# Pooled attention and routed experts on one core: q loaded behind the copies of k and q, row writes behind V's load, one send of maxima on GpSimd, one look at V later

## The chip, the core and the metric

The kernel runs on one core of a Trainium2 chip. The time is device microseconds of one execution. Three runs of the kernel before gave 1505.59, 1509.64 and 1510.80 us, so the median is 1509.64 us. The profile is of one more execution, which took 1513.62 us.

A core has these engines, each with an instruction stream of its own: TensorE (PE, with the weight loads shown apart as PEld), VectorE (DVE), ScalarE (ACT), GpSimd (POOL) and SyncE (SP), which here only issues DMAs. ACT and POOL issue some DMAs too. An engine takes its stream in order: an instruction that waits holds everything behind it.

## The reference

```python
def _attn_ref(q, k, v):                       # 8 batches, 8 heads, 1152 rows, 64 columns
    q_pool = q.reshape(B, H, S // 2, 2, D).mean(axis=3)       # 576 pooled queries
    scores = scale * np.matmul(q_pool, k.transpose(0, 1, 3, 2))
    scores = scores - np.max(scores, axis=-1, keepdims=True)
    attn = np.exp(scores)
    attn = attn / (np.sum(attn, axis=-1, keepdims=True) + 1e-09)
    return np.matmul(attn, v)

def _moe_ref(x, w_gate, w_output_gate, w1, w2):  # 4608 tokens of 512, 8 experts, hidden 1024
    logits = x @ w_gate
    e_idx = np.argmax(logits, axis=1)
    gate_w = softmax(logits)[np.arange(N), e_idx]
    eom = 1.0 / (1.0 + np.exp(-(x @ w_output_gate)))
    for e in range(E):
        mask = e_idx == e
        h = np.maximum(x[mask] @ w1[e], 0.0)
        out[mask] = gate_w[mask, None] * eom[mask, e, None] * (h @ w2[e])
```

Attention makes 4608 token rows. Each row then goes through the one expert that its gate picks.

## The kernel before

**Attention, by pairs.** Two heads of a batch are a pair: there are 32 pairs, four to a batch. The loop over `s` in `attention` takes 18 steps for a pair. In step `s`, TensorE makes the scores of one chunk of 128 keys against 576 queries (`sps`, lines 393 and 395, two accumulating groups), one or two matmuls of the *next* pair for its row maxima (`mp`, line 330), and in some steps a burst of `av` matmuls of an earlier chunk (lines 424 to 426, `ALAG` = 6 steps later). ScalarE takes two exponentials of each `sps` tile, either to `p` and `ph` (lines 407 and 408; GpSimd subtracts them to `pl` on line 409) or to `ph` and back into the tile (lines 399 and 400; VectorE subtracts on line 403). There are two `sps` buffers, so the scores of chunk c+2 wait for the readers of chunk c.

**Maxima.** VectorE reduces each `mp` tile (line 331). The maxima of a pair come in two groups, query tiles 0 to 4 and 5 to 8. A group is transposed by TensorE (line 365), split into two rows `mr` (lines 370, 371), and two small DMAs send these rows into `qb` (`send`, line 376, through `dmaf`, line 125), where the score matmul of line 395 subtracts them. `sends` runs them at the start of a step. Before the change ScalarE's stream issues all of them, 128 in 64 twos.

**Preparation of a pair**, by the tables `PREPF` (pair 0), `PREP0` (pair 1) and `PREP` (the others); a number in a table is a third of a step. `lk` loads q (`qp`, line 150) and k (`kpf`, line 151). GpSimd adds the two q rows that are pooled (`qsum`, line 235, into `yq`); ScalarE rounds k (`xk`, line 229) and q (`xq`, line 238); GpSimd makes the remainders (`kp` line 232, `yq` line 241). Twelve DMAs from SBUF to SBUF then lay these parts out for the matmuls: four `ka` of 288 KB, four `qa` or `qb` from `xq` of 144 KB, two `qa` from `yq` of 144 KB and two `kb` of 288 KB, 2592 KB in all, each of them through `dmaf`. They are called the copies below. `lv` loads V (`vp`, line 225) behind the k load that was issued last. `amax` (line 267, ScalarE) sums the absolute values of V of a head for a scale; `gmax` (line 272, TensorE) adds these over partitions; `vh`, `vs` and `vl` scale and split V into `vt`.

**Order.** PE, DVE, ACT and POOL take their instructions in the order in which the code calls them (`manual_schedule`). SP's order is a scheduler's: it places a DMA by when it thinks that its buffer is free. `qp`, `kpf` and `vp` have one buffer each. The DMAs that SP and ACT issue take eight semaphores in turn, so each such DMA, before it is issued, waits until the one eight places earlier on that list has landed. DMAs that GpSimd issues have eight semaphores of their own.

**Router.** After a batch's fourth pair, `logits` and `router` choose the experts, one piece per step or two. `wr` writes the batch's token rows to DRAM: 512 of them in one DMA of 1026 KB (line 575) and 64 in another of 128 KB (line 576). The index scatter has five parts (`t`), three steps apart; `wr` is called after the third.

**Experts.** Then come tiles of up to 256 tokens of one expert: gather of rows (line 750), `hps` (line 913), `yp` (lines 941 to 946), scatter.

Of the kernel before, what the change touches and what calls it, by code (L numbers as in the profile page):

```python
# [21 lines left out]
LS = 0  # L22
RI = 7
PREP0 = ((0, 'lk'), (6, 'qsum'), (10, 'kh', 0), (11, 'qh'), (12, 'kh', 1), (13, 'ql'), (14, 'kl'), (13, 'dq', 0), (14, 'dq', 1), (17, 'qd'), (21, 'sk', 0, 0), (24, 'sk', 0, 1), (27, 'sk', 1, 0), (30, 'sk', 1, 1), (23, 'dl', 0), (24, 'dl', 1),
        (53, 'lv'), (71, 'amax', 0), (74, 'amax', 1), (81, 'gmax'), (82, 'scale', 0), (85, 'scale', 1), (90, 'scale', 2), (93, 'vh', 0), (93, 'vs', 0), (96, 'vh', 1), (97, 'vl', 0), (100, 'vs', 1), (104, 'vl', 1))
PREPF = ((0, 'lf'), (1, 'fsel'), (3, 'qsv'), (4, 'kh', 0), (5, 'kh', 1), (6, 'klh', 0), (7, 'klh', 1), (8, 'sk', 0, 0), (9, 'sq0'), (10, 'sk', 0, 1), (11, 'sl', 0, 0), (13, 'qd'),
         (45, 'sl', 0, 1), (46, 'sk', 1, 0), (48, 'sk', 1, 1), (51, 'sq1'), (54, 'sl', 1, 0), (57, 'sl', 1, 1), (56, 'lv'),
         (78, 'amax', 0), (82, 'amax', 1), (99, 'gmax'), (100, 'scale', 0), (100, 'scale', 1), (100, 'scale', 2), (103, 'vh', 0), (103, 'vs', 0), (106, 'vh', 1), (107, 'vl', 0), (109, 'vs', 1), (113, 'vl', 1))
# [38 lines left out]
def attention(tc, qT, kT, vL, wg, keep, xrows, idscr, cum, pairs, setup, scat, init, exps):  # L67
    nc = tc.nc
    nb = len(pairs) // 4
    with ExitStack() as ctx:  # L70
# [51 lines left out]
            VTs.append(vt)  # L122

        def dmaf(o, i, q=nc.sync):
            q.dma_start(out=o.bitcast(F32), in_=i.bitcast(F32))

        lastk, sel, shn = [None], [], [0]

        def prep(n, table):

# [16 lines left out]
            gm = []  # L147

            def lk():
                nc.sync.dma_start(out=qp, in_=qT[b, hp].rearrange("p (t n) -> p t n", t=2))  # L150
                lastk[0] = nc.sync.dma_start(out=kpf, in_=kT[b, hp])


# [68 lines left out]

            def lv():
                with tc.issue_after(lastk[0].ins):
                    nc.sync.dma_start(out=vp, in_=vL[b, hp].rearrange("p (c d) -> p c d", d=64))

            def kh(i):
                z = slice(i * NQ, i * NQ + NQ)
# [30 lines left out]
            def dl(h):  # L259
                r = slice(64 * h, 64 * h + 64)  # L260
                o = h * (NQ + 64)
                dmaf(qa[64:128, o:o + NQ], yq[r])
                dmaf(kb[0:64, h], kp[r])

            def amax(h):
                j = sm.tile([128, NC, 64], F16, name="junk", bufs=1)
# [93 lines left out]
        def rows(force=False):  # L360
            while pend_t and (force or now[0] >= pend_t[0][-1] + TLAG):
                m9, nt, t0, t1, qbf, _ = pend_t.pop(0)
                tp, tk = psum(True)
                tp = tp[0:nt, 0:128]
                nc.tensor.transpose(out=tp, in_=m9[:, 0:nt], identity=ident)
                mr = sm.tile([5, 2, 128], F32R, name="mr")[0:nt]
                c0 = 16.0 * SHIFT

                def split(tp=tp, tk=tk, mr=mr, qbf=qbf, t0=t0, t1=t1, nt=nt):
                    nc.vector.tensor_scalar(out=mr[:, 0], in0=tp, scalar1=c0, scalar2=None, op0=ALU.subtract)  # L370
                    nc.vector.scalar_tensor_tensor(out=mr[:, 1], in0=tp, scalar=c0, in1=mr.bitcast(F32)[:, 0], op0=ALU.subtract, op1=ALU.subtract)
                    free(tk)

                    def send():
                        for j in range(2):
                            dmaf(qbf[66 + j:67 + j, 128 * t0:128 * t1].rearrange("o (t n) -> o t n", n=128), mr[:, j], nc.scalar)
                    pendd.append((send, now[0]))
                if now[0] < 18:
                    split()
                else:  # L380
                    pendv.append(split)
# [125 lines left out]
        def router(b, xb):  # L507
# [64 lines left out]

            def wr():
                r0 = b * NQ
                nc.sync.dma_start(out=xrows[r0:r0 + 512].rearrange("(t p) n -> p t n", p=128), in_=xb[:, 0:4])
                nc.sync.dma_start(out=xrows[r0 + 512:r0 + NQ], in_=xb[64:128, 4])
            if b == nb - 1:
                wr()
# [10 lines left out]
            for t in range(5):  # L589
# [5 lines left out]
                for q in scat:  # L595
                    tc.declare_no_dep(i.ins, q, reason="distinct slots")
                scat.append(i.ins)
                if t == 2 and b < nb - 1:
                    wr()
            if b == max(nb - 3, 0):  # L600
                yield from setup(psum, free)
# [640 lines left out]
```

## Time and profile before

| | |
|---|---|
| runs | 1505.59, 1509.64, 1510.80 us |
| profiled execution | 1513.62 us, span of its instructions 1511.9 us |
| mean granted TensorE clock | 0.987 |
| attention | to about 1000 us of the span, 32 pairs |
| change from attention to experts | about 1000 to 1060 us |
| experts | from about 1060 us to the end |
| largest load of the DMA engines | queue q1 (SP's), 241.52 MB |

The rows of the profile are read as follows. A row of the timeline has start, duration, engine, line, operation, what it writes and reads, and in brackets the engine's idle time before it with what ended it. "SPq" and "ACTq" are DMA issues by SP and ACT, and "x2" there is two of them with whatever lies between. A row of the windows gives, for a stretch of time, the busy time of each engine, the granted TensorE clock and what the DMA engines moved. A row of the waits gives who waited for whom, with total, times and longest.

### The profile page before, as it was taken

To read this page: it belongs to the slowest core of one execution; us is meant where nothing else is said; L and a number is where in the kernel's file an instruction comes from. 1 tells how busy PE (TensorE), PEld (TensorE's weight loads), DVE (VectorE), ACT (ScalarE), POOL (GpSimd) and SP (SyncE) were. 2 spreads that over 40 slices of the span, in tenths; PEclk is the share of its full clock that TensorE was granted. 3 is DMA by queue.
4 is the path that set the end of the run, shared out by engine and by line. 5 is a ranking of instruction groups with operands and counts; after the bars stand their busy time and mean duration, and the time that the engine had idled before them with its cause. 6 is when DMAs were issued, how large, how long until landed. Compare 5 with 4: busy or idle time off the path is not lost.

```text
span 1511.9 us, 40870 instructions
## 1 busy us (share of the span) xinstructions
PE 1469.9 (97%) x15806; PEld 1338.4 (89%) x15806; DVE 1100.0 (73%) x2359; ACT 1123.7 (74%) x1957; POOL 1014.0 (67%) x896
## 2 busy tenths in 40 slices
PE   7999999999999999999999999997999999999998
PEld 6989999999999999999899999985888888888985
DVE  7667777786777677777677777747778777787863
ACT  6778888888888888888788888884556556556662
POOL 5877888888888889878888998887233323333410
PEclk9999999999999999999999999997999999999999
DMA  5567665675566656665557655447966667446761
GB/s 170 137 160 183 164 153 140 164 172 150 135 167 168 157 135 153 173 166 152 136 140 176 168 141 154 101 149 257 354 235 214 227 234 234 164 174 240 254 218 67
DMA packets 96659, 265.95 MB, mean 176 GB/s; under 512 B 12778, under 2 KB 17018, under 8 KB 96450
## 3 DMA queue, kind: packets, MB, share of 16 engines
q1 hardware_dynamic: 85994, 241.52, 57.0%
q0 software_dynamic: 9024, 20.85, 3.9%
q8 instruction: 128, 2.10, 0.6%
q10 hardware_dynamic: 1440, 0.89, 0.2%
q14 instruction: 73, 0.60, 0.1%
HBM read 164.23 MB, written 22.50 MB: 124 GB/s over the span
## 4 chain that ended last, share of the span: by engine, by line
PE 91%; DVE 4%; ACT 2%; DMA 1%; POOL 1%; issue 1%; ACTq 0%; POOLq 0%; DVEq 0%; SPq 0%
PE mp L330 20%; PE hps L913 14%; PE sps L393 11%; PE sps L395 10%; PE av L424 6%; PE av L425 6%; PE av L426 6%; PE yp L943 4%; PE yp L944 4%; PE yp L946 4%; DVE pm L331 2%; PE tp L479 1%; PE xps L892 1%; PE tp L496 1%; PE yp L941 1%
## 5 line engine op out<-in xcount | busy, mean ns | idle before, releaser
L331 DVE TENSOR_REDUCE pm<-mp 128x1 f32<-128x384 f32 x864 | 452.4, 550 | 218.3 <-PE mp L330 217.3
L409 POOL TENSOR_TENSOR pl<-p,ph 128x576 f16<-128x576 f32 x386 | 494.1, 1286 | 153.0 <-ACT ph L408 119.8
L407 ACT ACTIVATE p<-sps 128x576 f32<-128x576 f32 x386 | 252.8, 655 | 104.6 <-PE sps L395 62.6
L330 PE MATMUL mp<-ka,qa 128*128 128x384 f32 x960 | 315.4, 345 | 0.0
L424 PEld LDWEIGHTS <-ph 128*128 128x128 f16 x2880 | 263.2, 97 | 39.7 <-issue 30.1
L424 PE MATMUL av<-vt,ph 128*128 128x65 f16 x2880 | 296.5, 194 | 0.0
L425 PE MATMUL av<-vt,ph 128*128 128x64 f16 x2880 | 294.4, 195 | 0.0
L426 PE MATMUL av<-vt,pl 128*128 128x65 f16 x2880 | 293.5, 193 | 0.0
L393 PE MATMUL sps<-qa,ka 128*128 128x288 f32 x1152 | 279.6, 324 | 10.9 <-ACT ph L408 7.0
L425 PEld LDWEIGHTS <-ph 128*128 128x128 f16 x2880 | 266.0, 97 | 0.8
L426 PEld LDWEIGHTS <-pl 128*128 128x128 f16 x2880 | 266.3, 99 | 0.0
L330 PE MATMUL mp<-kb,qb 66*128 66x384 f32 x768 | 261.3, 340 | 0.9 <-DVE kb L204 0.6
L408 ACT ACTIVATE ph<-sps 128x576 f16<-128x576 f32 x386 | 251.4, 651 | 0.0
L395 PE MATMUL sps<-qb,kb 68*128 68x288 f32 x1152 | 248.2, 297 | 0.0
L913 PE MATMUL hps<-x,w1h 128*128 128x512 f32 (+2 forms) x704 | 223.3, 381 | 2.1 <-DVE x L897 2.1
L393 PEld LDWEIGHTS sps<-qa,ka 128*128 128x128 f32 x1152 | 184.9, 192 | 15.7 <-ACT ph L408 9.9
L395 PEld LDWEIGHTS sps<-qb,kb 68*128 68x128 f32 x1152 | 187.0, 191 | 0.0
L330 PEld LDWEIGHTS mp<-ka,qa 128*128 128x128 f32 x960 | 179.0, 191 | 1.7 <-DVE pm L331 1.5
L913 PE MATMUL hps<-x,w1l 128*128 128x256 f32 (+2 forms) x704 | 162.6, 272 | 0.0
L915 ACT COPY hs<-hps 128x512 f32<-128x512 f32 (+2 forms) x88 | 47.4, 538 | 152.8 <-PE hps L913 144.4
L403 DVE TENSOR_TENSOR pl<-sps,ph 128x576 f16<-128x576 f32 x190 | 143.5, 755 | 16.9 <-ACT sps L400 12.9
L399 ACT ACTIVATE ph<-sps 128x576 f16<-128x576 f32 x190 | 124.4, 655 | 40.2 <-PE sps L395 31.6
(258 smaller groups left out, 2933.4 us busy)
## 6 DMA issues: line engine op xcount, KB each, us to landing
ka<-xk SPq DMA_DIRECT2D x120, 288.0 KB
raw1b<-in_w_dram SPq DMA_DIRECT2D x24, 1024.0 KB
raw2b<-in_w_dram SPq DMA_DIRECT2D x24, 1024.0 KB
raw1a<-in_w_dram SPq DMA_DIRECT2D x22, 1024.0 KB
raw2a<-in_w_dram SPq DMA_DIRECT2D x22, 1024.0 KB
vp<-in_vL_dram SPq DMA_DIRECT2D x32, 576.0 KB
qp<-in_qT_dram SPq DMA_DIRECT2D x31, 576.0 KB
kpf<-in_kT_dram SPq DMA_DIRECT2D x31, 576.0 KB
```

The lines of the kernel that those rows point to most:

```text
L330: nc.tensor.matmul(mp, lhsT=l, rhs=r, start=j == 0, stop=j == len(ops) - 1)
L331: nc.vector.tensor_reduce(out=pm[:, i:i + 1], in_=mp, axis=AX.X, op=ALU.max)
L393: nc.tensor.matmul(sps[:, j, 0:288], lhsT=ka[:, h, ks], rhs=qa[:, o + 288 * j:o + 288 * j + 288], start=True, stop=False)
L395: nc.tensor.matmul(sps[:, j, 0:288], lhsT=kb[:, h, ks], rhs=qb[:, h, 288 * j:288 * j + 288], start=False, stop=True)
L403: nc.vector.tensor_tensor(out=pl.rearrange("p (j n) -> p j n", j=2), in0=x, in1=ph2, op=ALU.subtract)
L407: nc.scalar.activation(out=p32.rearrange("p (j n) -> p j n", j=2), in_=x, func=AF.Exp, scale=1.0 / 16)
L408: e_ = nc.scalar.activation(out=ph2, in_=x, func=AF.Exp, scale=1.0 / 16)
L409: nc.gpsimd.tensor_tensor(out=pl, in0=p32, in1=ph, op=ALU.subtract)
L424: nc.tensor.matmul(av_[:, qb, 0:65], lhsT=hi, rhs=vt[:, h, c, 0:65], start=c == 0 and qb == 0, stop=False)
L425: nc.tensor.matmul(av_[:, qb, 0:64], lhsT=hi, rhs=vt[:, h, c, 66:130], start=False, stop=False)
L426: nc.tensor.matmul(av_[:, qb, 0:65], lhsT=lo, rhs=vt[:, h, c, 0:65], start=False, stop=c == NC - 1 and qb == 4)
L913: nc.tensor.matmul(hp[:, f, 0:n], lhsT=W1[l][g][:, c, fs], rhs=d['x'][:, c, 0:n], start=c == 0 and l == 0, stop=c == 3 and l == 0)
```

## The change

Five edits. `lk` issues q's load only after the last copy (`kb`) of the pair before it in the preparation. `wr` issues the write of 512 rows only after the V load that was called last, for all batches but the last, and is called after the fifth part of the scatter rather than the third. The send of maxima for query tiles 5 to 8 is issued by GpSimd when it comes up before step 9, which is so for pair 0 alone. In `PREP0`, the two `amax` of pair 1 come five thirds of a step later. The rest keeps the handles that this needs.

```diff
 PREP0 = (...
-        (53, 'lv'), (71, 'amax', 0), (74, 'amax', 1), (81, 'gmax'), (82, 'scale', 0), ...
+        (53, 'lv'), (76, 'amax', 0), (79, 'amax', 1), (81, 'gmax'), (82, 'scale', 0), ...
...
         def dmaf(o, i, q=nc.sync):
-            q.dma_start(out=o.bitcast(F32), in_=i.bitcast(F32))
-
-        lastk, sel, shn = [None], [], [0]
+            return q.dma_start(out=o.bitcast(F32), in_=i.bitcast(F32))
+
+        lastv = [None]
+        lastk, lastl, sel, shn = [None], [], [], [0]
...
             def lk():
-                nc.sync.dma_start(out=qp, in_=qT[b, hp].rearrange("p (t n) -> p t n", t=2))
+                with tc.issue_after(lastl[0].ins) if lastl else ExitStack():
+                    nc.sync.dma_start(out=qp, in_=qT[b, hp].rearrange("p (t n) -> p t n", t=2))
                 lastk[0] = nc.sync.dma_start(out=kpf, in_=kT[b, hp])
...
             def lv():
                 with tc.issue_after(lastk[0].ins):
-                    nc.sync.dma_start(out=vp, in_=vL[b, hp].rearrange("p (c d) -> p c d", d=64))
+                    lastv[0] = nc.sync.dma_start(out=vp, in_=vL[b, hp].rearrange("p (c d) -> p c d", d=64))
...
                 dmaf(qa[64:128, o:o + NQ], yq[r])
-                dmaf(kb[0:64, h], kp[r])
+                lastl[:] = [dmaf(kb[0:64, h], kp[r])]
...
                         for j in range(2):
-                            dmaf(qbf[66 + j:67 + j, ...], mr[:, j], nc.scalar)
+                            dmaf(qbf[66 + j:67 + j, ...], mr[:, j], nc.gpsimd if t0 and now[0] < 9 else nc.scalar)
...
             def wr():
                 r0 = b * NQ
-                nc.sync.dma_start(out=xrows[r0:r0 + 512].rearrange("(t p) n -> p t n", p=128), in_=xb[:, 0:4])
+                with tc.issue_after(lastv[0].ins) if b < nb - 1 else ExitStack():
+                    nc.sync.dma_start(out=xrows[r0:r0 + 512].rearrange("(t p) n -> p t n", p=128), in_=xb[:, 0:4])
                 nc.sync.dma_start(out=xrows[r0 + 512:r0 + NQ], in_=xb[64:128, 4])
...
-                if t == 2 and b < nb - 1:
+                if t == 4 and b < nb - 1:
                     wr()
```

The changed file is up to three lines longer, so a line such as 150 is 152 there, and 575 is 578. TensorE's and VectorE's streams hold the same instructions in the same order. The streams of SP, ACT and POOL change.

SP's stream in the first batches, at a pair with no row write beside it. `qp`, `kpf` and `vp` are the loads of q, k and V; the rows between them are the copies of one pair. Before:

```order
L225 DMA vp<-in_vL_dram 128x1152
L150 DMA qp<-in_qT_dram 128x1152
L125 DMA ka_121<-xk_5153 64x1152 x4
L125 DMA qa_124<-xq 64x576
L125 DMA qb_127<-xq 64x576
L125 DMA qa_124<-xq 64x576
L125 DMA qb_127<-xq 64x576
L125 DMA qa_124<-yq 64x576
L125 DMA kb_118<-kp_5149 64x1152
L125 DMA qa_124<-yq 64x576
L125 DMA kb_118<-kp_5149 64x1152
L151 DMA kpf<-in_kT_dram 128x1152
```

And after the change, the same pair:

```order
L227 DMA vp<-in_vL_dram 128x1152
L125 DMA ka_121<-xk_5153 64x1152 x4
L125 DMA qa_124<-xq 64x576
L125 DMA qb_127<-xq 64x576
L125 DMA qa_124<-xq 64x576
L125 DMA qb_127<-xq 64x576
L125 DMA qa_124<-yq 64x576
L125 DMA kb_118<-kp_5149 64x1152
L125 DMA qa_124<-yq 64x576
L125 DMA kb_118<-kp_5149 64x1152
L152 DMA qp<-in_qT_dram 128x1152
L153 DMA kpf<-in_kT_dram 128x1152
```

The load of the following pair's q stood ahead of twelve copies and stands behind them now; k's load keeps its place.

In the pairs where a batch's rows are written (seven of them), q's load stood behind the copies already before the change: there the order was V's load, the write of 512 rows, the copies, the write of 64 rows, q's load, k's load, V's load. After the change it is V's load, the write of 64 rows, the copies, q's load, k's load, V's load, the write of 512 rows.

ScalarE's stream in the first steps, at the second send of pair 0 (`qb_127<-mr`). Before:

```order
L408 ACTIVATE ph<-sps_430 128x576
L125 DMA qb_127<-mr 1x4x128 x2
L399 ACTIVATE ph<-sps_453 128x576
L400 ACTIVATE sps_453<-sps_453 128x2x288
L407 ACTIVATE p_481<-sps_476 128x576
```

After:

```order
L410 ACTIVATE ph<-sps_430 128x576
L401 ACTIVATE ph<-sps_453 128x576
L402 ACTIVATE sps_453<-sps_453 128x2x288
L409 ACTIVATE p_481<-sps_476 128x576
L410 ACTIVATE ph<-sps_476 128x576
```

The two DMAs are gone from here. They stand in GpSimd's stream now, behind the subtraction for chunk 0 (`pl<-p_435,ph`):

```order
L411 TENSOR_TENSOR pl<-p_435,ph 128x576
L125 DMA qb_127<-mr 1x4x128 x2
L411 TENSOR_TENSOR pl<-p_481,ph 128x576
L291 TENSOR_SCALAR vp<-vp,sc 128x576
L294 TENSOR_TENSOR vt_138<-vp,vt_138 128x9x64
```

ScalarE's stream some nine steps later, where the two `amax` of pair 1 (`junk,am<-vp`) stand. Before:

```order
L267 ACTIVATE junk,am<-vp 128x576
L407 ACTIVATE p_710<-sps_705 128x576
L408 ACTIVATE ph<-sps_705 128x576
L267 ACTIVATE junk,am<-vp 128x576
L238 CAST xq<-yq 128x576
L399 ACTIVATE ph<-sps_756 128x576
L400 ACTIVATE sps_756<-sps_756 128x2x288
L125 DMA qb_128<-mr 1x5x128 x2
```

After:

```order
L409 ACTIVATE p_708<-sps_703 128x576
L410 ACTIVATE ph<-sps_703 128x576
L240 CAST xq<-yq 128x576
L269 ACTIVATE junk,am<-vp 128x576
L401 ACTIVATE ph<-sps_754 128x576
L402 ACTIVATE sps_754<-sps_754 128x2x288
L269 ACTIVATE junk,am<-vp 128x576
L125 DMA qb_128<-mr 1x5x128 x2
```

The first moves behind one pair of exponentials and the rounding of q, the second behind the next pair of exponentials.

More of the change, by code (lines that the diff above doesn't have):

```diff
@@ L24 @@
 PREP0 = ((0, 'lk'), (6, 'qsum'), (10, 'kh', 0), (11, 'qh'), (12, 'kh', 1), (13, 'ql'), (14, 'kl'), (13, 'dq', 0), (14, 'dq', 1), (17, 'qd'), (21, 'sk', 0, 0), (24, 'sk', 0, 1), (27, 'sk', 1, 0), (30, 'sk', 1, 1), (23, 'dl', 0), (24, 'dl', 1),
-        (53, 'lv'), (71, 'amax', 0), (74, 'amax', 1), (81, 'gmax'), (82, 'scale', 0), (85, 'scale', 1), (90, 'scale', 2), (93, 'vh', 0), (93, 'vs', 0), (96, 'vh', 1), (97, 'vl', 0), (100, 'vs', 1), (104, 'vl', 1))
+        (53, 'lv'), (76, 'amax', 0), (79, 'amax', 1), (81, 'gmax'), (82, 'scale', 0), (85, 'scale', 1), (90, 'scale', 2), (93, 'vh', 0), (93, 'vs', 0), (96, 'vh', 1), (97, 'vl', 0), (100, 'vs', 1), (104, 'vl', 1))
 PREPF = ((0, 'lf'), (1, 'fsel'), (3, 'qsv'), (4, 'kh', 0), (5, 'kh', 1), (6, 'klh', 0), (7, 'klh', 1), (8, 'sk', 0, 0), (9, 'sq0'), (10, 'sk', 0, 1), (11, 'sl', 0, 0), (13, 'qd'),
@@ L375, in send @@
                         for j in range(2):
-                            dmaf(qbf[66 + j:67 + j, 128 * t0:128 * t1].rearrange("o (t n) -> o t n", n=128), mr[:, j], nc.scalar)
+                            dmaf(qbf[66 + j:67 + j, 128 * t0:128 * t1].rearrange("o (t n) -> o t n", n=128), mr[:, j], nc.gpsimd if t0 and now[0] < 9 else nc.scalar)
                     pendd.append((send, now[0]))
```

## The prediction

> **What bounds the kernel now.** I read the page first, then the windows by stage, then what TensorE waits for, and then ScalarE's and SyncE's timelines at those waits.
>
> ```profile
> span 1511.9 us, 40870 instructions
> PE 1469.9 (97%) x15806; PEld 1338.4 (89%) x15806; DVE 1100.0 (73%) x2359; ACT 1123.7 (74%) x1957; POOL 1014.0 (67%) x896
> PEclk9999999999999999999999999997999999999999
> ...
> 0.00:100.00 100.00, 87.14 (x870) 79.66 (x871) 68.29 (x149) 69.24 (x126) 65.82 (x90) 0.91 0.60 161
> 100.00:1000.00 900.00, 889.16 (x12095) 839.68 (x12091) 668.87 (x1692) 763.04 (x1410) 761.29 (x662) 1.00 0.61 151
> 1000.00:1060.00 60.00, 48.63 (x471) 40.89 (x471) 36.49 (x103) 35.93 (x59) 47.93 (x37) 0.86 0.75 265
> 1060.00:1511.90 451.90, 444.95 (x2381) 378.15 (x2379) 326.32 (x418) 255.51 (x364) 138.94 (x110) 1.00 0.63 217
> ```
>
> TensorE is the bound, and its instructions are the same after the change. So time can come only from its idle time and from stretches at a lower clock. The change reaches the first two rows: 12.9 us idle of the first 100 with a mean clock of 0.91, and 10.8 us idle of the next 900. The stage of the experts is not reached. What ends TensorE's idle time:
>
> ```profile
> PE tp L272 <- ACT junk L267: 2.4, 1, 2.4
> PE sps L393 <- DVE pl L403: 2.3, 3, 1.6
> ...
> PE sps L393 <- ACT ph L408: 6.7, 6, 2.3
> ```
>
> The first two rows are of the first 100 us, the third of 100 to 1000. In all three ScalarE was late. Three of these gaps have a price beyond themselves, since the granted clock is halved behind them:
>
> ```profile
> 30.90:41.10 10.20, 9.88 (x59) 9.32 (x60) 4.64 (x9) 7.15 (x12) 8.29 (x8) 0.50 0.17 57
> 88.90:95.70 6.80, 6.80 (x49) 6.49 (x50) 1.75 (x5) 3.36 (x6) 3.50 (x4) 0.50 0.96 259
> 740.90:744.30 3.40, 3.40 (x36) 3.10 (x37) 0.56 (x1) 2.88 (x5) 3.29 (x3) 0.50 0.99 252
> ```
>
> They stand behind the gaps of 1.6, 2.4 and 2.3 us. The other five gaps of the 6.7 us have 4.4 us together, 0.9 each, and no lower clock behind them. Half-clock time that TensorE fills costs half of its length: 5.1, 3.4 and 1.7 us.
>
> **What makes ScalarE late** is the sends of maxima that it issues:
>
> ```profile
> 27.74 1.30 ACTq L125 DMA_DIRECT2D qb<-mr  x2
> 83.76 3.14 ACTq L125 DMA_DIRECT2D qb<-mr  x2
> 242.10 1.97 ACTq L125 DMA_DIRECT2D qb<-mr  x2
> 736.34 3.26 ACTq L125 DMA_DIRECT2D qb<-mr  x2
> ...
> 334.64 0.70 ACTq L125 DMA_DIRECT2D qb<-mr  x1
> 335.43 0.69 ACTq L125 DMA_DIRECT2D qb<-mr  x1
> ```
>
> A plain send of two takes 1.3 to 1.5 us. At 83.76, 242.10 and 736.34 the second one waited 1.6, 0.5 and 1.8 us longer. It needs the semaphore of the DMA eight places earlier, which is one of the large `ka` copies. SyncE's rows around it:
>
> ```profile
> SPq L150 <- POOL yq L235: 139.6, 23, 7.3
> ...
> 233.18 0.33 SPq L150 DMA_DIRECT2D qp<-in_qT_dram  x1
> 233.61 3.75 SPq L125 DMA_DIRECT2D ka<-xk  x4
> ...
> 245.41 1.34 SPq L151 DMA_DIRECT2D kpf<-in_kT_dram  x1
> ...
> 337.89 1.36 SPq L150 DMA_DIRECT2D qp<-in_qT_dram  x1
> 339.30 0.44 SPq L151 DMA_DIRECT2D kpf<-in_kT_dram  x1
> ...
> 356.99 0.33 SPq L150 DMA_DIRECT2D qp<-in_qT_dram  x1
> ...
> 233.20:245.40 12.20, 11.54 (x137) 10.77 (x135) 9.98 (x27) 9.61 (x20) 9.37 (x9) 1.00 0.95 215
> ```
>
> In 23 pairs q's load sits in SyncE's stream until GpSimd has read the old q, and goes out just ahead of the copies, as at 233.18. It is 576 KB, and the DMA engines then move 215 GB/s, so it holds every copy back by up to 2.7 us. In a pair with a row write, as at 334.64, q goes out after the copies (337.89), and there the two sends stand 0.79 us apart, with no wait between. This case already holds the rearrangement, though with 1026 KB of rows ahead of the copies.
>
> **The change, part by part.**
>
> *q behind the copies.* Removed from ahead of them are 2.7 us of DMA time, more than any of the waits above (1.8 us at most). So the waits go, and with them the 6.7 us of gaps between 100 and 1000 us and the 1.7 us of half clock: **8.4 us**. At 83.76 go the gap of 2.4 us and 3.4 us of half clock, 5.8 us. The second of these sends comes to wait for the fourth `ka` instead of the third, which eats part of the margin, and I take **5.5 us**. Bounds: nothing, if the copies delay one another without q, and 14.2 us together. What is late next: q and k now leave together, at about 245.4 in the pair above. They are 1152 KB, 5.5 us at 215 GB/s, and are used when GpSimd reads q. The rows at 337.89 and 356.99 give the room: the next q is let out 19.1 us after the last one was, behind that read of 1.4 us. So some 12 us are left, and I take nothing for it. Behind q in SyncE's stream stand k's load, which was behind the copies already, and V's load, some 10 us later.
>
> *Row writes.* The rows for this:
>
> ```profile
> SPq L575 <- DVE xb L571: 32.9, 7, 4.7
> ...
> 349.30:357.00 7.70, 7.70 (x125) 7.36 (x122) 5.24 (x13) 6.60 (x14) 7.33 (x8) 1.00 0.27 81
> ```
>
> SyncE waits for the rows' last column as before, 4.7 us each, now with the small write; the copies behind it needed this time anyway, since in a pair without a write they also start about 8 us after V's load. The large write, 1026 KB or 4.9 us at 215 GB/s, moves into the stretch behind V's load, where the DMA engines are at 0.27. It costs nothing, and gains at most the share that it held of the copies' time, which no gap of TensorE shows. If that cover were gone, it would delay the next copies like q did, by 1 to 2 us in seven pairs.
>
> *The second send of pair 0 on GpSimd.* The rows at the start:
>
> ```profile
> 27.39 0.43 PE L395 MATMUL sps<-qb,kb 68*128 68x288 f32 x2
> 29.09 0.65 ACT L399 ACTIVATE ph<-sps 128x576 f16<-128x576 f32 x1 [1.28 <-DVE tp L277]
> 30.31 0.76 DVE L403 TENSOR_TENSOR pl<-sps,ph 128x576 f16<-128x576 f32 x1 [0.39 <-ACT sps L400]
> 31.22 0.82 PE L393 MATMUL sps<-qa,ka 128*128 128x288 f32 x2 [1.55 <-DVE pl L403]
> ...
> 29.10:39.90 10.80, 9.25 (x45) 8.37 (x44) 5.93 (x12) 8.32 (x15) 7.17 (x8) 0.58 0.31 100
> ```
>
> The scores of chunk 1 are there at 27.82, but ScalarE starts on them at 29.09, behind its send. VectorE and TensorE follow in a chain. Without the send this chain is 1.24 us earlier and the gap 0.3 us, so the half clock at 30.9 goes too. Its 5.1 us are not all won. From 29.1 to 39.9 ScalarE has 8.3 us of work. Packed without gaps from 27.85 it ends at 36.2 instead of 39.9. So I take **3.7 us**, with 1.2 (the half clock stays) and 6.4 (all of 1.24 and 5.1) as bounds. GpSimd now issues the two DMAs:
>
> ```profile
> L592 POOL DMA_INDIRECT idscr<-tid,posi x40: 977/1063/1203, 209.0 to 1034.2; - x40
> ...
> 27.89 1.28 POOL L409 TENSOR_TENSOR pl<-p,ph 128x576 f16<-128x576 f32 x1 [4.89 <-ACT ph L408]
> 31.46 1.29 POOL L409 TENSOR_TENSOR pl<-p,ph 128x576 f16<-128x576 f32 x1 [2.29 <-DMA kpf<-in_kT_dram]
> ```
>
> No direct DMA of GpSimd is in the trace. Its indirect ones take 1.06 us, so two take 2.1 us, and GpSimd is idle for 2.29 us there. Bounds are 0 and 2.4 us (two of 1.2). Behind them wait the subtractions `pl`, which TensorE needs six steps later; the rows themselves are needed nine steps later. I take nothing for it.
>
> *V of pair 1 looked at later.*
>
> ```profile
> 48.36 0.69 ACT L267 ACTIVATE junk<-vp 128x576 f16<-128x576 f32 x1
> ...
> 50.12 0.35 PE L272 MATMUL tp<-am,onesf 128*128 128x2 f32 x2
> ```
>
> The second `amax` ends some 1 us ahead of the matmul that sums it, and moves behind two exponentials of 0.55 us each. TensorE may then wait up to 0.8 us there; the exponentials that it overtakes come 0.6 us earlier, which takes away a gap of 0.4 us (the 2.3 us of `pl` above less 1.6 are two such gaps). I take **0.4 us** as a cost (bounds: a gain of 0.4 and a cost of 0.8).
>
> **Sum**, against the profiled 1513.62 us: 8.4 + 5.5 + 3.7 − 0.4 = 17.2 us off, 1496.4 us. The median of the runs, 1509.64, lies 4.0 us below the profiled execution. The gap at 738 us and its half clock, 4.0 us, occur once in the trace and may be just that. They are gone after the change either way, so I keep **1496 us**.
>
> **Rivals.**
>
> *The copies delay one another without q.* Then the sends wait as before and only the start gains: 1513.62 − 3.7 + 0.4 = 1510.3 us. For it: at 242.10 the wait is for the fourth of four copies of 288 KB. Against it: the sends at 334.64 and 335.43.
>
> *The half clock has another cause than these gaps.* Then 1.24 + 2.4 + 6.7 − 0.4 = 9.9 us go and 1503.7 us stay. For it: the half clock at 30.9 begins 0.3 us before the gap's end, so the gap alone need not have set it. Against it: three of three long gaps have it, and five of five short ones don't. [...]
>
> *q comes late (slower).* Where q and k land later than the 12 us of room, GpSimd's sum of q, the copies and then the maxima of the next pair wait, and each microsecond of it counts in 23 pairs: 1496 + 23 = 1519 us for one. From a rate below some 70 GB/s on (1152 KB in 17 us) this decides. For it: two loads now share one slot. Against it: the seven pairs in which they did so already.
>
> *The change doesn't do what it says:* excluded for SyncE's order, which is known.
>
> **How the numbers follow.** The forecast (1490 to 1501 us) has 0.64, the other cause of half clock 0.12, the copies 0.10, q late 0.04. The remaining 0.10 is new short stalls, between 1501 and 1510. The range is 1489 to 1505 us: the forecast with the bounds of its unknown costs, the second rival, and half of the rest. A measurement of this kernel can tell some 0.3%, 4.5 us, from no change, so faster means below 1505.1: 0.64 + 0.12 + 0.05, or 0.81. The same has 0.15 (the copies and the other half of the rest), slower 0.04.
>
> **What would show it.** Right: sends of 1.3 to 1.5 us throughout, TensorE's wait for `ph` L408 between 100 and 1000 us under 1 us, a granted clock of 1.00 from 11 to 1000 us, and no second send in ScalarE's stream near 28 us. Wrong: sends that still take over 1.9 us, GpSimd idle ahead of L235 for q's load, half clock with no gap ahead of it, or a new wait of `sps` or `av` for `pl` in the first 60 us.

## The result, and the profile after

The changed kernel takes 1497.53 us (median of 6 runs, 1493.13 to 1499.76), the kernel before 1510.30 us in the runs beside it. The ratio is 0.9911, with a 95% interval of 0.9892 to 0.9929. The profiled execution took 1499.76 us, 13.9 us less than the profiled one of before.

The page of the changed kernel, and its windows by stage, with the columns as before. The last two rows are the stretch with a lower clock that is left in the attention, and the 3.4 us ahead of it:

```profile
span 1497.9 us, 40864 instructions
PE 1462.9 (98%) x15806; PEld 1331.9 (89%) x15806; DVE 1099.7 (73%) x2359; ACT 1123.0 (75%) x1957; POOL 1015.0 (68%) x898
PEclk9999999999999999999999999998999999999999
```

```profile
0.00:100.00 100.00, 88.76 (x958) 81.32 (x959) 72.97 (x160) 74.54 (x134) 72.29 (x97) 0.97 0.61 163
100.00:1000.00 900.00, 894.00 (x12187) 843.75 (x12186) 668.15 (x1688) 769.07 (x1425) 766.53 (x665) 1.00 0.61 155
...
47.50:54.30 6.80, 6.78 (x59) 6.48 (x60) 3.12 (x8) 3.51 (x6) 2.27 (x4) 0.50 1.03 237
44.10:47.50 3.40, 1.97 (x13) 1.57 (x12) 2.10 (x5) 2.72 (x8) 3.40 (x3) 1.00 0.94 202
```

What TensorE waited for, the first two rows between 0 and 100 us and the others between 100 and 1000:

```profile
PE sps L395 <- DVE pl L405: 1.7, 2, 1.1
PE tp L274 <- ACT junk L269: 1.4, 1, 1.4
...
PE tp L481 <- DVE pm L333: 2.1, 7, 0.3
PE sps L395 <- DVE pl L405: 1.6, 3, 0.7
PE sps L397 <- DMA qb<-mr: 0.5, 1, 0.5
```

The largest row of before, the 6.7 us for `ph` between 100 and 1000 us, is gone, and no stretch at half clock is left there. Still there is a wait for V's sum (`junk`), now at 46 us, and half clock behind it. The sends, from the timeline (the one at 724.82 answers to the one at 736.34 of before):

```profile
21.00 2.10 ACTq L125 DMA_DIRECT2D qb<-mr  x2
...
29.10 1.31 POOL L125 DMA_DIRECT2D qb<-mr  x2
...
63.70 0.62 ACTq L125 DMA_DIRECT2D qb<-mr  x1
...
112.54 0.71 ACTq L125 DMA_DIRECT2D qb<-mr  x1
...
724.82 0.70 ACTq L125 DMA_DIRECT2D qb<-mr  x1
725.61 0.69 ACTq L125 DMA_DIRECT2D qb<-mr  x1
...
981.30 0.60 ACTq L125 DMA_DIRECT2D qb<-mr  x1
```

At 724.82 the second follows the first by 0.79 us, where it came 2.58 us later before. The start of a send also marks the same place of the program in every kernel here, since each has all 64 twos in one order. So the attention is cut into three stretches by four sends: the first of pair 0, the second of pair 1, the first of pair 3 and the last one of pair 31. In the changed kernel these are the sends at 21.00, 63.70, 112.54 and 981.30 us. All kernels of this study, in us of their profiled executions (a profile is one execution), with the median and the ratio from all runs (each ratio is to the kernel before in the runs beside it, whose medians were 1509.33 to 1510.48 us):

| kernel | to pair 1's second send | to pair 3's first | to pair 31's last | median | ratio (95%) |
|---|---|---|---|---|---|
| before | 43.39 | 54.35 | 875.70 | 1510.30 | |
| changed | 42.70 | 48.84 | 868.76 | 1497.53 | 0.9911 (0.9892 to 0.9929) |
| q_only | 43.32 | 48.83 | 865.73 | 1498.60 | 0.9924 (0.9894 to 0.9953) |
| q_ahead | 39.65 | 48.84 | 887.86 | 1513.13 | 1.0027 (1.0005 to 1.0049) |
| send_only | 41.17 | 48.80 | 873.56 | 1506.63 | 0.9983 (0.9969 to 0.9996) |
| amax_back | 43.03 | 48.78 | 866.47 | 1496.26 | 0.9914 (0.9886 to 0.9943) |
| rows_back | 39.51 | 48.86 | 865.93 | 1494.12 | 0.9906 (0.9870 to 0.9943) |
| q_mixed | 41.69 | 48.85 | 866.88 | 1495.27 | 0.9916 (0.9884 to 0.9948) |
| sum_later | 39.11 | 48.85 | 867.37 | 1496.22 | 0.9913 (0.9886 to 0.9941) |
| fill_gap | 39.49 | 48.86 | 867.42 | 1496.01 | 0.9908 (0.9872 to 0.9944) |
| extra_copy | 39.88 | 48.85 | 869.51 | 1498.95 | 0.9920 (0.9898 to 0.9942) |
| sends_pool | 40.08 | 49.64 | 889.23 | 1517.57 | 1.0044 (1.0023 to 1.0065) |
| q_pair3 | 41.23 | 48.97 | 871.56 | 1499.04 | 0.9918 (0.9895 to 0.9941) |
| rows_sum | 39.11 | 48.97 | 867.10 | 1494.88 | 0.9892 (0.9870 to 0.9914) |

Of the 13.9 us between the two profiles, 0.7 lie in the first stretch, 5.5 in the second and 6.9 in the third; the rest lies behind them.

### The profile page after: what moved, and what is told of

Read it like the earlier page. It is cut to its first block, busy times and chain, and to the rows that moved or that the text cites. A ratio compares the mean times of both kernels' runs of the same rounds, so it can differ in the third digit from the quotient of the medians.

```text
span 1497.9 us, 40864 instructions
## 1 busy us (share of the span) xinstructions
PE 1462.9 (98%) x15806; PEld 1331.9 (89%) x15806; DVE 1099.7 (73%) x2359; ACT 1123.0 (75%) x1957; POOL 1015.0 (68%) x898
## 4 chain that ended last, share of the span: by engine, by line
PE 93%; DVE 3%; DMA 1%; issue 1%; ACT 1%; POOL 0%; ACTq 0%; POOLq 0%; SPq 0%; DVEq 0%
PE mp L332 21%; PE hps L916 14%; PE sps L395 12%; PE sps L397 10%; PE av L426 6%; PE av L427 6%; PE av L428 6%; PE yp L946 5%; PE yp L947 5%; PE yp L949 4%; DVE pm L333 1%; PE tp L481 1%; PE xps L895 1%; PE tp L498 1%; PE yp L944 1%
## 5 line engine op out<-in xcount | busy, mean ns | idle before, releaser
L426 PEld LDWEIGHTS <-ph 128*128 128x128 f16 x2880 | 262.6, 97 | 39.5 <-issue 29.2
```

Source lines behind the costliest of these rows:

```text
L426: nc.tensor.matmul(av_[:, qb, 0:65], lhsT=hi, rhs=vt[:, h, c, 0:65], start=c == 0 and qb == 0, stop=False)
```

## The experiments

### q alone behind the copies (q_only)

The kernel before with the edits of `dmaf`, `dl` and `lk`, and nothing else.

```diff
-                nc.sync.dma_start(out=qp, in_=qT[b, hp]...)
+                with tc.issue_after(lastl[0].ins) if lastl else ExitStack():
+                    nc.sync.dma_start(out=qp, in_=qT[b, hp]...)
```

> The kernel before, with one part of the change: the next q loaded behind the copies of k and q. Theory (the q edit carries nearly the whole gain; in the traces the two stretches behind the start gained 5.5 us at 86-94 us and about 7 us at 100-1000 us): 1510.3 - 12.5 = about 1498, ratio 0.990 to 0.993; the first send of pair 1 stays at 50.2 us, the half clock near 31 us stays, TensorE's waits for ph ahead of L393 between 100 and 1000 us are under 1 us in all, and no gap stands near 86 us. The recorded prediction's terms: 8.4 + 5.5 = 13.9 us off, 1496.4. Rival (the copies delay the sends by themselves, and the moved q is not the cause): the gaps of 0.6 to 2.3 us ahead of L393 stay, 1509 to 1511.

It takes 0.9924 of the kernel before, against 0.9911 for all edits. What TensorE waited for `ph` between 100 and 1000 us:

```profile
PE sps L394 <- ACT ph L409: 0.3, 1, 0.3
```

6.7 us in the kernel before are 0.3 us here, and the third stretch is 10.0 us shorter. The start is as before. The q edit carries nearly the whole gain, and the rival falls.

### q ahead again, the other parts changed (q_ahead)

```diff
-                with tc.issue_after(lastl[0].ins) if lastl else ExitStack():
-                    nc.sync.dma_start(out=qp, in_=qT[b, hp]...)
+                nc.sync.dma_start(out=qp, in_=qT[b, hp]...)
```

> The changed kernel with the next q loaded ahead of the copies again; the other three parts stay. Theory (q edit carries the gain): 1497.5 + 12 to 13 = about 1510; waits of 0.6 to 2.4 us ahead of L393 for ph return once in a pair where the sends stand behind the copies, sends take over 1.9 us again. Rival (the row writes or the moved sum of V have a share of it): 1500 to 1506.

The gain is gone: 1.0027, even a little over the kernel before. TensorE's waits between 100 and 1000 us, and from the timeline the send and the gap at 236 us:

```profile
PE sps L394 <- ACT ph L409: 12.2, 9, 2.8
```

```profile
225.24 0.33 SPq L151 DMA_DIRECT2D qp<-in_qT_dram  x1
225.67 3.35 SPq L125 DMA_DIRECT2D ka<-xk  x4
...
236.04 1.83 ACTq L125 DMA_DIRECT2D qb<-mr  x2
237.93 0.65 ACT L408 ACTIVATE p<-sps 128x576 f32<-128x576 f32 x1 [4.23 <-DVE sc L283]
239.17 0.85 PE L394 MATMUL sps<-qa,ka 128*128 128x288 f32 x2 [2.82 <-ACT ph L409]
```

ScalarE starts its exponentials behind the two sends, at 237.93, and TensorE goes on at 239.17. The start, though, took 39.65 us, 3.7 us less than before. So the send's gain is there when q stands ahead. In the third stretch this kernel is 14.3 us longer than send_only. There the edits differ in the row writes alone, but the order on SP differs in q as well. Its waits, here and in the kernel before:

```profile
SPq L151 <- POOL yq L236: 147.3, 29, 7.3
```

```profile
SPq L150 <- POOL yq L235: 139.6, 23, 7.3
```

So q's load stands ahead of the copies in six of the seven pairs that write rows too (send_only has 23 waits, as before). Of the 12.2 us of gaps, 10.7 follow the sends in the last pairs of the batches, whose copies come next behind the moved write; send_only has 4.5 us there.

### The send alone (send_only)

The kernel before with the `send` edit only.

```diff
-    dmaf(qbf[66 + j:67 + j, ...], mr[:, j], nc.scalar)
+    dmaf(qbf[66 + j:67 + j, ...], mr[:, j], nc.gpsimd if t0 and now[0] < 9 else nc.scalar)
```

> The kernel before, with one part of the change: the second maxima of pair 0 sent by GpSimd. Recorded prediction: 3.7 us off (1.2 to 6.4), so 1506.6: the half clock at 30.9 us goes, and TensorE's first score follows 1.2 us earlier. Theory read from the two traces (the start is worth about 4 us by 46 us of the span, and what it loses again lies in the moved sum of V): 1510.3 - 4 = about 1506, first send of pair 1 near 46 us in place of 50.2. Rival (ScalarE, whose sum of V stands early here, now waits for V's load, which does not come earlier by itself): a ScalarE wait of 1 us or more ahead of L269 between 38 and 45 us, a gap of TensorE behind it, and 1509 to 1511.

3.1 us less by the medians (0.9983), and a first stretch that is 2.2 us shorter in the profile. ScalarE's first sum of V, from the timeline:

```profile
45.70 0.69 ACT L267 ACTIVATE junk<-vp 128x576 f16<-128x576 f32 x1 [1.86 <-DMA vp<-in_vL_dram]
```

Both readings are partly right. The send's part is real, and 1.9 us of ScalarE's lead go to a wait for V's load. This kernel also lacks the gap at 86 us, though q stands ahead of the copies in it. q_ahead lacks it too.

### V's sums at their former place (amax_back)

```diff
-        (53, 'lv'), (76, 'amax', 0), (79, 'amax', 1), (81, 'gmax'), ...
+        (53, 'lv'), (71, 'amax', 0), (74, 'amax', 1), (81, 'gmax'), ...
```

> The changed kernel with the sums of V of pair 1 at their former places (71 and 74). Recorded prediction: 0.4 us faster (bounds: 0.8 us faster to 0.4 us slower), 1497.1. Theory A (the moved sum is what cost 1.45 us of gap and 3.4 us of half clock at 46 to 54 us): 1497.5 - 4.9 = 1492.6, no gap ahead of L274. Theory B (V's load lands at 44.9 us whatever the place, so ScalarE would stand waiting for it ahead of its exponentials): same to 2 us slower, 1497.5 to 1499.5, with a wait of ScalarE for the load of 1.5 to 3 us ahead of L269 and a gap of TensorE ahead of L395.

0.9914, the same as the changed kernel. Its timeline, and below it that of the changed kernel at the same place:

```profile
44.80 0.68 ACT L269 ACTIVATE junk<-vp 128x576 f16<-128x576 f32 x1 [2.68 <-DMA vp<-in_vL_dram]
```

```profile
44.92 0.68 ACT L269 ACTIVATE junk<-vp 128x576 f16<-128x576 f32 x1 [0.66 <-DMA vp<-in_vL_dram]
...
46.71 0.67 ACT L269 ACTIVATE junk<-vp 128x576 f16<-128x576 f32 x1
...
47.52 0.59 PE L274 MATMUL tp<-am,onesf 128*128 128x2 f32 x2 [1.45 <-ACT junk L269]
```

The sum starts when V's load lands, at 44.8 and 44.9 us, from both places in ScalarE's stream. Where it stands early, ScalarE waits 2.68 us ahead of it, and TensorE then waits 1.6 us for `ph` in place of 1.45 us for the sum. The half clock from 47.5 us on is in both. So the late load sets this loss, and the place of the sum only chooses who waits.

### The sum's matrix product later (sum_later)

```diff
-        (81, 'gmax'), (82, 'scale', 0), (85, 'scale', 1), (90, 'scale', 2), ...
+        (85, 'gmax'), (86, 'scale', 0), (88, 'scale', 1), (91, 'scale', 2), ...
```

> The changed kernel with the matrix product of V's sums and what follows it (the mask, the scale, the reciprocal) of pair 1 a few steps later (81, 82, 85, 90 become 85, 86, 88, 91); the sums themselves stay at 76 and 79. Theory A (TensorE stands 1.45 us at 46.07 us for the late sum, and half clock follows for 6.8 us): no gap ahead of that product, no half clock near 47 us, second send of pair 1 at 59 to 60.5 us in place of 63.7 (from the first send of pair 0), 1497.5 - 3.5 to 4.9 = 1492.6 to 1494. Rival (the wait moves to the scaled copies of V and to TensorE's product with them): same within 1 us, and a new gap behind 55 us.

The gap and the half clock are gone, and the first stretch is the shortest of all, 39.11 us. From the timeline:

```profile
47.27 0.51 PE L395 MATMUL sps<-qa,ka 128*128 128x288 f32 x2 [0.22 <-DVE pl L405]
...
48.60 0.28 PE L274 MATMUL tp<-am,onesf 128*128 128x2 f32 x2
```

TensorE now has scores to make ahead of the product. The median, 1496.22, is not told apart from the changed kernel's, since V's load came earlier here (the first sum began at 44.41 without a wait), so not all of the 3.6 us are due to this edit.

### One q ahead of nothing (q_mixed)

```diff
-                with tc.issue_after(lastl[0].ins) if lastl else ExitStack():
+                with tc.issue_after(lastl[0].ins) if lastl and n != 2 else ExitStack():
```

> The changed kernel, but the q of pair 2 (the one loaded while pair 1 is made ready) is loaded ahead of the copies again; all later ones stay behind them. Theory (q behind the copies let pair 1's ka copies start at 40.63 us in place of 42.15, beside V's load, which then landed too late for its sum; with q ahead the copies stay out of its way): V's sum without a wait, the gap ahead of the product 0.7 us as in the run with q ahead everywhere, no half clock near 47 us, second send of pair 1 near 60.7 us, later stretches as in the changed kernel: 1497.5 - 3 = 1494.5. Rival (the saving at the start is lost again at 86 us, where the kernel before had its 2.37 us gap): 1497 to 1500, with a half clock near 88 us.

The q of pair 2 was the wrong one. It is loaded at 24 us, ahead of any such copies, so that the order on every engine stays that of the changed kernel. The run tests nothing of the theory and is a second sample of the changed kernel: ratio 0.9916, and a first stretch of 41.69 us in place of 42.70. Its timeline, and its windows cut in stretches of 3.41 us counted from its half clock at 30.9 us, show how a start differs from one execution to the next:

```profile
46.63 0.68 ACT L269 ACTIVATE junk<-vp 128x576 f16<-128x576 f32 x1 [1.39 <-DMA vp<-in_vL_dram]
...
49.22 0.38 PE L274 MATMUL tp<-am,onesf 128*128 128x2 f32 x2 [2.18 <-ACT junk L269]
```

```profile
44.55:47.97 3.42, 2.49 (x21) 2.09 (x17) 1.65 (x5) 2.03 (x6) 3.42 (x3) 1.00 1.02 228
47.97:51.38 3.41, 2.16 (x39) 2.16 (x40) 1.30 (x3) 2.47 (x6) 2.15 (x2) 1.00 0.81 194
51.38:54.80 3.42, 3.22 (x33) 2.98 (x32) 3.19 (x9) 2.76 (x6) 1.69 (x4) 1.00 0.91 214
```

A longer gap, of 2.18 us, has no half clock behind it here (1.00 in all three rows); 0.93 us of it lie in one stretch and 1.25 in the next.

### TensorE kept busy ahead of the product (fill_gap)

Six more products, their result unused, ahead of pair 1's `gmax`.

```diff
+                if n == 1:
+                    f_ = psum(name="fill")
+                    for _ in range(6):
+                        nc.tensor.matmul(f_[:, 0:384], lhsT=ka[:, 0, 0:128], rhs=KAs[0][:, 0, 0:384], start=True, stop=True)
                 nc.tensor.matmul(g, lhsT=onesf, rhs=am, start=True, stop=True)
```

> The changed kernel with six more products (128x384 each, their result unused) on TensorE just ahead of pair 1's product of V's sums, where it stands idle for 1.45 us. Theory (that idle time makes the half clock at 47.5 us): no idle over 0.7 us there, no half clock behind it, second send of pair 1 about 3.4 us earlier than in the changed kernel (60 to 61 us), though the product itself comes no earlier than 47.5; 1497.5 - 3.4 = 1494.1. Rival (the half clock has another cause, and gaps of 1.5 us alone don't bring it): half clock at 47.5 us stays, 1497.5 or up to 1.5 us more.

No gap and no half clock, as the theory has it, but it isn't settled by this: V's load came early in this execution too. From its timeline:

```profile
46.37 0.68 ACT L269 ACTIVATE junk<-vp 128x576 f16<-128x576 f32 x1
...
47.92 1.24 PE L275 MATMUL fill<-ka,ka 128*128 128x384 f32 x6
...
48.99 0.36 PE L278 MATMUL tp<-am,onesf 128*128 128x2 f32 x2
```

Without the fill TensorE would have stood some 1.1 us (47.92 to 48.99), less than the 1.45 us of the changed kernel. That is about as long as in rows_back below, which has no half clock either. Inconclusive.

### The row writes at their former place (rows_back)

```diff
-                with tc.issue_after(lastv[0].ins) if b < nb - 1 else ExitStack():
-                    nc.sync.dma_start(out=xrows[r0:r0 + 512]...)
+                nc.sync.dma_start(out=xrows[r0:r0 + 512]...)
...
-                if t == 4 and b < nb - 1:
+                if t == 2 and b < nb - 1:
```

> The changed kernel with the router's row writes where they were before (at the third of five scatters, both writes ahead of V's load). Recorded prediction: the row writes are worth nothing, 1497.5 with 1 us either way (1496.5 to 1498.5), V's sums in the four pairs behind a batch without a wait. Rival (the large write ahead of V's load and of the copies delays them): 1 to 6 us slower, waits of TensorE for ph between 100 and 1000 us of over 0.6 us near 250, 370, 500 us.

0.9906 against 0.9911, with intervals that overlap, and 865.93 us in the third stretch against 868.76: the moved row writes bring nothing that can be told, and cost some 3 us at most in these profiles. TensorE's waits for `ph` are 0.3 us in all between 100 and 1000 us, so the rival falls. V's load landed earlier in its profile, and the gap ahead of the product was 0.92 us, without half clock:

```profile
47.06 0.38 PE L274 MATMUL tp<-am,onesf 128*128 128x2 f32 x2 [0.92 <-ACT junk L269]
```

Its first write of rows comes only at 188.94 us, so the start is the changed kernel's own, and the first stretch took 39.51 us. So the 42.70 us of the changed kernel are one outcome among several of the same order of instructions at the start.

### Bytes ahead of the copies (extra_copy)

One more copy from SBUF to SBUF, its result unused, ahead of each pair's `ka`.

```diff
+            ex_ = sq.tile([128, 896], F32R, name="extra")
...
+                if h == 0:
+                    dmaf(ex_, xk[:, 0:896])
                 dmaf(ka[0:64, h], xk[r])
```

> The changed kernel with one more copy (448 KB, its result unused) ahead of each pair's copies of k, so that bytes stand ahead of them again though q stays behind; the order of sends and copies on the queues' eight slots is the same. Theory (the sends wait until a ka copy eight transfers earlier has landed, and bytes ahead of the copies make it late): waits of TensorE for ph ahead of L395 between 100 and 1000 us of over 0.6 us again, in four pairs or more, second sends 0.4 us or more behind the first, 5 to 15 us slower than the changed kernel: 1502 to 1512. Rival (it was q's own place, not the bytes): 1496 to 1499.

The sends wait again, but the time hardly follows: 1498.95 us. TensorE's waits between 100 and 1000 us, and a send from the timeline:

```profile
PE sps L398 <- ACT ph L413: 2.6, 5, 1.1
```

```profile
724.08 0.70 ACTq L125 DMA_DIRECT2D qb<-mr  x1
...
726.60 0.69 ACTq L125 DMA_DIRECT2D qb<-mr  x1
...
728.58 0.53 PE L398 MATMUL sps<-qa,ka 128*128 128x288 f32 x2 [0.73 <-ACT ph L413]
```

Six second sends waited, 0.3 to 1.7 us each, about as long as in the kernel before (0.4 to 1.8 us). Yet there are only 2.6 us of gap, 2.1 of them behind such sends. What is missing are waits of the first sends, which the prediction did not count. A first send goes out some 0.5 us after its row of maxima (`mr`) is written, if nothing holds it. The last pair of the sixth batch in the kernel before, in the changed kernel and here, with the rounding of k (`xk`), the first issue of `ka` and the row of maxima:

```profile
723.78 0.69 ACT L229 CAST xk<-kpf 128x576 fp32r<-128x576 f32 x1
...
727.48 3.73 SPq L125 DMA_DIRECT2D ka<-xk  x4
...
734.03 0.27 DVE L370 TENSOR_SCALAR mr<-tp 5x128 fp32r<-5x128 f32 x1
```

```profile
713.74 0.69 ACT L231 CAST xk<-kpf 128x576 fp32r<-128x576 f32 x1
...
714.46 3.55 SPq L125 DMA_DIRECT2D ka<-xk  x4
...
724.08 0.27 DVE L372 TENSOR_SCALAR mr<-tp 5x128 fp32r<-5x128 f32 x1
```

```profile
723.33 0.27 DVE L375 TENSOR_SCALAR mr<-tp 5x128 fp32r<-5x128 f32 x1
```

The send of this row went at 736.34 before, 2.04 us after the row, at 724.82 after the change and at 724.08 here, both some 0.5 us after it. So before, the first send waited 1.6 us and the second 1.8 us, and here the second alone waited 1.7 us. In the nine gaps for `ph` that follow such sends in these two kernels, the gap is the sum of the two waits less 1.0 us each time (3.3 and 2.3 us before, 1.7 and 0.7 here).

The first sends waited since the copies started late, and this is the second part of q's effect. In the kernel before, q's load waits in SP's stream for GpSimd (`SPq L150 <- POOL yq L235`, 139.6 us in 23 waits), with the copies behind it. In the last pairs of the second to seventh batch the first `ka` was issued 2.97 to 3.03 us after the rounding of k had ended, and 0.03 us after it in the changed kernel. From that issue until the maxima were there, these pairs had 6.8 to 8.0 us before, and 9.7 to 10.8 in the changed kernel. Their first sends waited 0.5 to 1.6 us before; here, with 9.2 to 10.4 us, two of the six waited, by 0.5 us. The extra copy has 448 KB where q has 576, so the share of the bytes is measured only roughly.

### The first maxima sent by GpSimd (sends_pool)

q_ahead, with the first send of each pair from pair 2 on moved off ScalarE.

```diff
-    nc.gpsimd if t0 and now[0] < 9 else nc.scalar
+    nc.gpsimd if (t0 and now[0] < 9) or (t0 == 0 and now[0] >= 18) else nc.scalar
```

> The kernel with the next q ahead of the copies again and the other parts changed (1513.1 as measured, with gaps of 1.17 to 2.82 us ahead of L394), with the first maxima of each pair from pair 2 on sent by GpSimd in place of ScalarE. Theory (ScalarE is held by its own send, which waits for a copy to land): gaps of over 0.6 us for ph between 100 and 1000 us are gone, 1513.1 - 12 to 15 = 1498 to 1501. Rival (the DMA engines are full then, 86% busy in q_ahead's 225-245 us, so that a send through any engine lands late): TensorE waits for qb ahead of L396 by the same 1 to 3 us, 1510 to 1514. Third: GpSimd's queue is late, its waiting sends hold back the pl and kl work behind them: slower, 1503 to 1515, with waits for pl.

The waits for `ph` are gone, as the first reading has it, but 14.5 us of waits for the sends themselves stand in their place, as the second reading has it. The time, 1517.57 us, is longer than any of the three readings said. Waits between 100 and 1000 us, and one case from the timeline:

```profile
PE sps L396 <- DMA qb<-mr: 14.5, 14, 3.1
```

```profile
202.61 1.09 POOL L125 DMA_DIRECT2D qb<-mr  x2
...
210.96 0.50 PE L396 MATMUL sps<-qb,kb 68*128 68x288 f32 x2 [1.79 <-DMA qb<-mr]
```

Two transfers of 2.5 KB, both issued by 203.70, were not both there before 210.9, with the DMA engines at 187 GB/s in these 8 us. Another sender doesn't help here. Whether the engines alone make these transfers late, or GpSimd's own queue too, on which an index scatter stands at 204.00, isn't separated: ScalarE's two sends of the same pair in q_ahead, the second issued at 204.00, cost TensorE no wait that is listed there.

### The right q ahead (q_pair3)

```diff
+                with tc.issue_after(lastl[0].ins) if lastl and n != 3 else ExitStack():
```

> The changed kernel, but one q, that of pair 3 (loaded at 41.7 us where q stood ahead, beside V's load of pair 1), ahead of the copies again. Theory (with that q ahead the copies start 1.5 us later and V's load lands in time for its sum): no wait of ScalarE for V, a gap of 0.7 us ahead of the product of V's sums, first send of pair 0 to second send of pair 1 39.7 us as in q_ahead (42.7 in the changed kernel's trace, 41.7 in q_mixed's), other gaps as in the changed kernel: 1495 to 1496. Rival (the two orders differ there only by chance from run to run, as rows_back's 39.5 us shows): a wait for V of 0.5 to 1.5 us ahead of the sum again, time the same.

V's sum came without a wait, with a gap of 0.69 us, as in q_ahead. But late copies then held TensorE themselves:

```profile
58.05 0.41 PE L332 MATMUL mp<-kb,qb 66*128 66x384 f32 x1 [1.36 <-DMA kb<-kp]
```

The first stretch took 41.23 us. So V's load won 0.8 us of gap and the half clock here, and pair 2's maxima lost 1.4 us. That loss isn't steady: with the same order at this place, q_ahead has no such wait and sends_pool one of 0.5 us. The time, 1499.04 us, is above the 1495 to 1496 expected. Its profile also has three waits of TensorE for the sends themselves between 100 and 1000 us, 2.7 us together, and half clock behind the longest, of 1.65 us, at 518 us.

### Both best starts (rows_sum)

rows_back with sum_later's table.

```diff
-        (81, 'gmax'), (82, 'scale', 0), (85, 'scale', 1), (90, 'scale', 2), ...
+        (85, 'gmax'), (86, 'scale', 0), (88, 'scale', 1), (91, 'scale', 2), ...
...
-                if t == 4 and b < nb - 1:
+                if t == 2 and b < nb - 1:
```

> The changed kernel with the row writes at their former place and the product of pair 1's V sums a few steps later, the two that came out lowest at the start: no half clock between 20 and 1000 us, first send of pair 0 to second send of pair 1 39.1 us, no gap over 1.1 us between 20 and 1000 us. If the time follows that: 1494 to 1495.5, 2 to 3 us under the changed kernel. If the start's 3 us are lost in other runs to the place of the gap: 1496 to 1498, the same as the changed kernel.

1494.88 us, 0.9892 (0.9870 to 0.9914). Its first stretch of 39.11 us is sum_later's. It is the lowest ratio, but its interval overlaps the changed kernel's, so it isn't shown to be faster.

## Why the prediction was right, and where not

*The time and the bound.* 1496 us were forecast and 1497.53 measured, inside the forecast's own 1490 to 1501. The gain came from TensorE's idle time and its clock in the first 1000 us, as the first two rows of windows had it. That the forecast lies so near is in part luck: 17.2 us were taken off the profiled execution, and 13.9 came off between the profiles, but that execution of the kernel before stood 3.3 us above its median.

*q behind the copies, 8.4 us.* Right in size: 10.0 us of the third stretch in q_only and 6.9 in the changed kernel. Its working had one cause, the 2.7 us of bytes, and set them against the second sends' waits of 1.8 us at most. With the first sends' waits ScalarE was held by up to 3.3 us, so this comparison doesn't carry the forecast. extra_copy shows that bytes alone bring only 2.6 us of gap. The rest is the hold in SP's stream, whose row (139.6 us in 23 waits) the prediction quoted but priced at nothing: without it the copies of the last pairs start 3.0 us sooner. No run has this hold without the bytes, so its share isn't measured by itself.

*The 5.5 us at 84 us.* They went in the trace (54.35 to 48.84 us), but also in send_only and q_ahead, where q stands ahead. The step took a loss seen in one profile for q's steady price. By the medians q_only gains 1509.75 − 1498.60 = 11.2 us in place of 13.9, so some of this may be chance of that execution, as the prediction itself suspected of the 4.0 us at 738. It may also hang on the start, which is another in send_only and q_ahead; no run separates the two.

*The second send, 3.7 us.* Right, and a little more. From the first send of pair 0 to the first of pair 1 there are 29.2 us in the two kernels whose second send is ScalarE's (before and q_only). They are 25.0 us in eleven of the twelve others, and 26.4 in q_mixed, which still had 3.4 us of half clock at 30.9. The forecast of its gap was off, 1.05 us where 0.3 were said, because VectorE's subtraction still ends late. GpSimd's two DMAs took 1.31 us, as long as ScalarE's same two (1.30 at 27.74) and below the 2.1 estimated, and delayed nothing that TensorE waited for.

*V looked at later, cost 0.4 us.* This is the step that failed. Its bounds were −0.4 and +0.8 us, and the profile shows a gap of 1.45 us and 6.8 us of half clock behind it, which cost another 3.4: 4.9 us. The prediction's own sign of a granted clock of 1.00 from 11 to 1000 us failed with it. The step compared the sum's end with TensorE's product in a trace in which V's load was in time. Where it is in time after the change too, the gap is 0.69 us, within the bounds (q_ahead, q_pair3, extra_copy, sends_pool). amax_back shows that the moved sum isn't the cause of the rest. With the send gone, pair 1's first maxima are sent 4.2 us earlier (46.00 after 50.20), but V's load is issued only 1.5 us earlier (39.02 after 40.55), so it takes the place of the send at the head of the chain.

V's load also takes longer, 5.9 us from its issue to the last update of its semaphore where it took 3.7 before. This goes with the copies, which now start 1.6 us behind it. In all seven kernels in which `ka` starts 1.6 us behind V's load, it took 5.3 to 6.6 us; with 3.0 us it took 5.0 us in three and 3.7 in one, and with 4.3 us (before, q_only) 3.7. So the q edit probably adds to the loss. That isn't shown, since no run changes this alone, and extra_copy, with its own copy 1.6 us behind V's load, took 3.6. In other executions V lands some 0.5 us sooner and nearly all of the loss is gone (rows_back). The start's forecast of 3.7 − 0.4 = 3.3 us became 0.7 in this profile, 1.7 in q_mixed's and 3.9 in rows_back's.

*Row writes, nothing.* Right as far as can be told where q stands behind: rows_back has 0.9906 and the changed kernel 0.9911. With q ahead again the moved writes do cost: 14.3 us in the third stretch and 6.5 us in the medians (q_ahead against send_only). The price named for a lost cover, 1 to 2 us in seven pairs, can't be read from this alone, since q's load moves ahead of the copies in six pairs with the same edit.

*The rivals.* "The copies delay one another without q" falls with q_only. "q comes late" falls too: neither TensorE nor GpSimd waits for q's load between 60 and 1000 us. "The half clock has another cause" falls as well. In the fourteen profiles, between 15 and 1000 us, I summed TensorE's idle time in each stretch of 3.41 us, counted from where a half clock began. That is the length of the half clock from 740.88 to 744.29 us in the kernel before. All 12 stretches with 1.45 us or more were followed by half clock, none with 1.02 or less, and 4 of 15 in between, so the bound isn't sharp: 1.06 us brought it once (q_mixed, at 27.45) and 1.44 us once didn't (sends_pool, at 337.89). The length of a gap alone doesn't tell the cases apart: the changed kernel's 1.45 us lie in one stretch (the row at 44.10, with 1.97 of 3.40 us busy) and the next row, at 47.50, has 0.50, while q_mixed's 2.18 us, split over two, have 1.00 behind them.

*What stays open:* why V's load takes 5.9 us from its issue in one execution of the same order of instructions (39.02 to 44.92) and 6.6 in another (q_mixed, 39.99 to 46.63), how much of the second stretch's 5.5 us the kernel before loses on average, and why a send still lands late now and then with q behind the copies (0.5 us of wait in the changed kernel's profile, 2.7 in q_pair3's).

## What to carry to other kernels

Look for a load that waits for its buffer with transfers that are ready behind it, and put it behind those. Here q's load waited 139.6 us in 23 waits, and behind it the first copy in the last pairs of six batches was issued some 3.0 us after its data was there, against 0.03 us after the change; the move was worth 0.8% (q_only). When an engine issues several transfers in a row, look at the wait of each: here the first one's was left out, and it made up more than half of the delay (7.8 of 12.5 us in the last pairs of six batches of the kernel before). Before crediting a chain with the removal of its late member, look for the next one: which load feeds this place, and does its issue move as far? A loss that one profile shows at one place should be looked for in a second execution before it is booked in full.

## What the runs showed of the hardware

Two direct DMAs took GpSimd 1.31 us to issue (29.10 in the changed kernel), and the same two took ScalarE 1.30 (27.74 in the kernel before). Two transfers of 2.5 KB took over 7 us to land while the DMA engines moved 187 GB/s (sends_pool, 203 to 211 us).

The granted clock went to 0.50 behind 1.45 us of idle time in one stretch of 3.41 us (changed kernel, 47.5 us), and stayed at 1.00 behind 2.18 us over two (q_mixed, 0.93 and 1.25). Between 15 and 1000 us the half clocks of the kernel before last 10.24, 6.83 and 3.41 us, from 30.91, 88.93 and 740.88 us on, and that of the changed kernel 6.83 us, from 47.52 on. The three in the kernel before begin 58.02 and 651.95 us after one another, 17 and 191 times a third of 10.24 us. Counted from the half clock of each, a stretch begins at 44.11 us in the changed kernel and at 44.55 in q_mixed, whose order of instructions is the same. And the same place met a gap with half clock in one of these executions and without in the other: near 30 us the changed kernel has a gap of 1.05 us without it, split 0.8 and 0.25 over two stretches, and q_mixed one of 1.06 us with it, all in one.
